# Moving one chunk's attention steps among the first FFN groups of a fused retention and gated FFN kernel

## The chip, the cores and the metric

The kernel runs on one core of a Trainium2 chip. The metric is the device time of one execution in microseconds (us). An execution of the kernel before was also profiled; all times of single instructions below come from that one profile. The engines are named as in it: PE is TensorE (matrix products; PEld is its loading of weights), DVE is VectorE, ACT is ScalarE, POOL is GpSimd, SP is SyncE.

## The reference

Two stages follow each other. The first is a retention recurrence over four sequences of 768 steps with 8 heads of width 64; the second is a feed-forward network (FFN) with a sigmoid gate over the 3072 tokens that result.

```python
gamma = 1.0 - 2.0 ** (-5.0 - np.arange(H))
for t in range(S):
    state = gamma * state + outer(k[:, :, t], v[:, :, t])      # per batch and head, 64 x 64
    y[:, :, t] = scale * q[:, :, t] @ state
x = y.transpose(0, 2, 1, 3).reshape(3072, 512)
out = (sigmoid(x @ w_gate) * (x @ w_val)) @ w_out              # 512 -> 1536 -> 512
```

## The kernel before

**Chunks.** The recurrence is computed in chunks of 128 steps, numbered g = 0 to 23, six for each sequence. A chunk passes through these functions:

- `transposes_early(g)` (L150 to L159): for k and then for q, four TensorE transposes of 128x128 (L158) into PSUM and one ScalarE copy (L159) into the tile `qkT`. `transposes` (L146, L148) does the same with one copy and is used from chunk 4 on.
- `scale_v(g)` (L169): v times a decay table, into `vs`, on VectorE or GpSimd.
- `scores(g)` (L179): eight products of k and q. `masks(g)` (L184, L185): two VectorE products with the causal mask, into `stA` and `stB`.
- `inter(g)` (L191): four products of q with the state of the chunk before, into the PSUM tile `y`.
- `state(g)` (L201): eight products of k and `vs` added to the state. `state_out(g)` (L209): two ScalarE copies of the state into `zbd`.
- `intra(g)` (L215): eight products of `vs` with `stA` and `stB`, added to `y`.
- `y_out(g)` (L223): one VectorE product of `y` with a decay table, into 128 columns of `xT`, the input of the FFN.

**FFN.** Four chunks make an FFN tile t of 512 tokens. `up(t, n1, lo, hi)` computes one of twelve groups for the columns lo to hi: four products with `wg` and four with `wv` (L261), a sigmoid on ScalarE (L265) and a VectorE product (L266) into `hT`. `up_columns` (L275, L280, L281) does several groups for few columns. `down(t, sm, part)` (L292) is half of a 128-row block of the output product, six matmuls; behind the second half ScalarE copies the block (L297), and SP stores it.

**PSUM.** The tiles of tag `ff` rotate through three buffers. `keep_on`, each half of an `up`, the q part of `transposes_early` and each `down` block take the next one in the order of the program. The first product into a buffer waits until its last content has been read.

**Order.** The schedule is manual: each engine runs its instructions in the order in which the program issues them. The lines up to L389 are written out one after the other. `keep_on(n)` (L304) issues n products of the identity with itself into an unused `ff` tile. Behind them the loop over t issues 9 `up` groups and 8 `down` halves for t = 0, numbered 0 to 16, and places the nine steps of chunks 4 to 7 behind the groups named in `place`. The last of these, `step_y(6, 7)`, issues `inter(6)`, `scores(7)`, `state(6)`, `intra(6)`, `state_out(6)`, `masks(7)` and `y_out(6)`. The first group of t = 1 is `up(1, 0, 0, 384)`, which reads the columns of chunks 4, 5 and 6.

**Loads.** The loads of k, q and v (L67, L68, L62), `wg` and `wv` (L81) and `wo` (L85) are issued on GpSimd's queue in a fixed order; a slab of `wg` or `wv` holds two groups.

Of the kernel before, what the change touches and what calls it, by code (L numbers as in the profile page):

```python
# [17 lines left out]
def kernel(  # L18
# [51 lines left out]
    def load_chunk(g):  # L70
        load_kq(g)
        load_v(g, nc.gpsimd)
# [66 lines left out]
    def pair(t, p):  # L139
        return t[:, 2 * p:2 * p + 2, :].rearrange("s h d -> s (h d)")  # L140
# [9 lines left out]
    def transposes_early(g):  # L150
        qkT[g] = at.tile([128, 2 * NP, C], BF16, tag="qkT", name="qkT", bufs=3)
        for i, x in enumerate((kn[g], qn[g])):
            if i:
                tp = pf.tile([128, NP, C], BF16, tag="ff", name="tq", padded_shape=[128, 2 * NP, C])
            else:
                tp = pa.tile([128, NP, C], BF16, tag="tp", name="tp", padded_shape=[128, 2 * NP, C])
            for p in range(NP):
                nc.tensor.transpose(tp[:, p, :], pair(x, p), ident)  # L158
            nc.scalar.activation(qkT[g][:, i * NP:(i + 1) * NP], tp, AX.Copy)  # L159
# [7 lines left out]
    def scale_v(g, eng):  # L167
        vs[g] = ld.tile([C, H, D], BF16, tag="vs", name="vs", bufs=4)
        eng.tensor_tensor(vs[g], vf[g], tabv[:, g % NCH, :].unsqueeze(2).to_broadcast([C, H, D]),  # L169
                          op=ALU.mult)  # L170

    def scores(g):
        t = qkT[g]
        sc[g] = (pa.tile([128, NP, C], F32, tag="sA", name="sA"),
                 pa.tile([128, NP, C], F32, tag="sB", name="sB"))
        for p in range(NP):
            for i in range(2):
                half = slice(i * D, (i + 1) * D)
                nc.tensor.matmul(sc[g][i][:, p, :], t[half, p, :], t[half, NP + p, :], start=True, stop=True)  # L179

    def masks(g):
        stA[g] = at.tile([128, NP, C], BF16, tag="stA", name="stA")
        stB[g] = at.tile([128, NP, C], BF16, tag="stB", name="stB")
        nc.vector.tensor_tensor(stA[g], sc[g][0], causal4, op=ALU.mult)  # L184
        nc.vector.tensor_tensor(stB[g], sc[g][1], causal4, op=ALU.mult)  # L185

    def inter(g):
        y[g] = pa.tile([128, NP, C], F32, tag="y", name="y")
        if g % NCH > 0:
            for p in range(NP):  # L190
                nc.tensor.matmul(y[g][:, p, :], zbd[(g - 1) % 2][:, p, :], qkT[g][:, NP + p, :],  # L191
                                 start=(p == 0), stop=False, skip_group_check=True)

    def state(g):
        b, c = divmod(g, NCH)
        if c == 0:
            zps[b] = pa.tile([128, NP, D], F32, tag="z", name="z", padded_shape=[128, NP, C])
        if c < NCH - 1:
            for p in range(NP):
                for i in range(2):  # L200
                    nc.tensor.matmul(zps[b][i * D:(i + 1) * D, p, :], kn[g][:, 2 * p + i, :], vs[g][:, 2 * p + i, :],  # L201
                                     start=(c == 0 and p == 0), stop=True, skip_group_check=True)

    def state_out(g):
        b, c = divmod(g, NCH)
        if c < NCH - 1:
            for i in range(2):
                half = slice(i * D, (i + 1) * D)
                nc.scalar.copy(zbd[g % 2][half, :, half], zps[b][half])  # L209

    def intra(g):
        first = g % NCH == 0
        for p in range(NP):
            for i, st in enumerate((stA[g], stB[g])):
                nc.tensor.matmul(y[g][i * D:(i + 1) * D, p, :], vs[g][:, 2 * p + i, :], st[:, p, :],  # L215
                                 start=(first and p == 0), stop=True, skip_group_check=True)

    def y_out(g):
        c = g % NCH
        if g % 4 == 0:  # L220
            xT[g // 4] = at.tile([128, NP, 512], BF16, tag="xT", name="xT")
        col = (g % 4) * C
        nc.vector.tensor_tensor(xT[g // 4][:, :, col:col + C], y[g], taby[:, :, c * C:(c + 1) * C], op=ALU.mult)  # L223

    def step_t(g):
        if g < XBAR:
            transposes(g)
        scale_v(g, nc.vector if g < XBAR else nc.gpsimd)

    def step_s(g):  # L230
        scores(g)
        masks(g)
# [21 lines left out]
    def up(t, n1, lo=0, hi=512):  # L254
        if t not in hT:
            hT[t] = ffn.tile([128, NFF, 512], BF16, tag="hT", name="hT", bufs=2)
        ps = []
        for w in (wg, wv):
            u = pf.tile([128, 512], F32, tag="ff", name="ff")
            for kk in range(KT):  # L260
                nc.tensor.matmul(u[:, lo:hi], w[:, kk, n1 * 128:(n1 + 1) * 128], xT[t][:, kk, lo:hi],  # L261
                                 start=(kk == 0), stop=(kk == KT - 1))
            ps.append(u)
        gs = ffn.tile([128, 512], F32, tag="gs", name="gs")
        nc.scalar.activation(gs[:, lo:hi], ps[0][:, lo:hi], AX.Sigmoid)  # L265
        nc.vector.tensor_tensor(hT[t][:, n1, lo:hi], gs[:, lo:hi], ps[1][:, lo:hi], op=ALU.mult)  # L266

    def up_columns(t, n1s, lo, hi):
        n = hi - lo
        ps = []  # L270
        for w in (wg, wv):
            u = pf.tile([128, 512], F32, tag="ff", name="ff")
            for i, n1 in enumerate(n1s):
                for kk in range(KT):
                    nc.tensor.matmul(u[:, i * n:(i + 1) * n], w[:, kk, n1 * 128:(n1 + 1) * 128], xT[t][:, kk, lo:hi],  # L275
                                     start=(kk == 0), stop=(kk == KT - 1))
            ps.append(u[:, :len(n1s) * n])
        gs = ffn.tile([128, 512], F32, tag="gs", name="gs")
        g = gs[:, :len(n1s) * n]
        nc.scalar.activation(g, ps[0], AX.Sigmoid)  # L280
        nc.vector.tensor_tensor(hT[t][:, n1s[0]:n1s[-1] + 1, lo:hi], g.rearrange("p (i n) -> p i n", n=n),  # L281
                                ps[1].rearrange("p (i n) -> p i n", n=n), op=ALU.mult)
# [18 lines left out]
    def keep_on(n):  # L301
        u = pf.tile([128, 512], F32, tag="ff", name="ff")
        for _ in range(n):
            nc.tensor.matmul(u[:, :128], ident, ident, start=True, stop=True)  # L304
# [64 lines left out]
    scores(2)  # L369
    masks(2)  # L370
    inter(2)
    state(2)
    state_out(2)
    keep_on(12)
    intra(2)
    y_out(2)
    scale_v(3, nc.vector)
    transposes_early(3)
    up(0, 0, 0, 384)
    scores(3)  # L380
    masks(3)
    inter(3)
    state(3)
    state_out(3)
    up(0, 1, 0, 384)
    intra(3)
    y_out(3)
    up(0, 2, 0, 384)
    up_columns(0, range(3), 384, 512)  # L389


    def ups(t):
        return [lambda n1=n1: up(t, n1) for n1 in range(NFF)]

    def downs(t):
        return [lambda sm=sm, i=i: down(t, sm, i) for sm in range(4) for i in range(2)]

    for t in range(NT):
        groups, steps, place = ups(t) + downs(t), [], []
        if t == NT - 1:  # L400
            groups[-2:] = [lambda: last_down(t)]
        if t == 0:
            groups = groups[3:]
            steps = [lambda: step_t(4), lambda: step_s(4), lambda: step_y(4), lambda: step_t(5), lambda: step_s(5),
                     lambda: step_t(6), lambda: step_y(5, 6), lambda: step_t(7), lambda: step_y(6, 7)]
            place = [5, 6, 8, 10, 11, 12, 13, 14, 15]
        elif t + 1 < NT:
            steps = attention(t + 1)
            place = [0, 1, 3, 5, 7, 8, 10, 13, 17]
        if t == 1:  # L410
            groups[:2] = [lambda: up(1, 0, 0, 384), lambda: step_y(7), lambda: up(1, 1, 0, 384),
                          lambda: up_columns(1, range(2), 384, 512)]
            place = [p + 2 for p in place]
        if t + 2 < NT:
            for g in range(4 * t + 8, 4 * t + 12):
                load_chunk(g)
        for i, group in enumerate(groups):
            if i == len(groups) - 9:
                for g in range(4 * t + 8, 4 * t + 12):
                    if XBAR <= g < NG:  # L420
                        xbar(g)
            group()
            for p, step in zip(place, steps):
                if p == i:
                    step()
# [30 lines left out]
```

## Time and profile before

| What | us |
|---|---|
| median of 7 runs | 237.27 (237.04 to 237.88) |
| profiled execution | 237.16 |
| its span, first to last instruction | 235.5 |
| PE busy in the span | 225.9 (96%) |
| DVE busy | 104.5 |
| ACT busy | 90.8 |
| POOL busy | 92.1 |

The span is what the instructions of the profile cover; the profiled execution's own time is 1.66 us above it. The granted TensorE clock was 1.000 of full speed in the mean. In a line of the timeline the first number is the start in us from the start of the span, the second the time that the piece covers, then the engine, the line of the kernel, the operation, output and input tiles with their shapes, and the number of instructions; a bracket tells how long the engine had been idle, and what ended the wait. [...]pieces overlap: the cost of a piece in a full stream is the distance from its start to the start of the next.

### The profile page before, as it was taken

To read this page: it belongs to the slowest core of one execution; us is meant where nothing else is said; L and a number is where in the kernel's file an instruction comes from. 1 tells how busy PE (TensorE), PEld (TensorE's weight loads), DVE (VectorE), ACT (ScalarE), POOL (GpSimd) and SP (SyncE) were. 2 spreads that over 40 slices of the span, in tenths; PEclk is the share of its full clock that TensorE was granted. 3 is DMA by queue.
4 is the path that set the end of the run, shared out by engine and by line. 5 is a ranking of instruction groups with operands and counts; after the bars stand their busy time and mean duration, and the time that the engine had idled before them with its cause. 6 is when DMAs were issued, how large, how long until landed. Compare 5 with 4: busy or idle time off the path is not lost.

```text
span 235.5 us, 4300 instructions
## 1 busy us (share of the span) xinstructions
PE 225.9 (96%) x1702; PEld 117.8 (50%) x1728; DVE 104.5 (44%) x178; ACT 90.8 (39%) x173; POOL 92.1 (39%) x111
## 2 busy tenths in 40 slices
PE   6869999999999999999999999999999999999994
PEld 5646544555555554445454444445444554444444
DVE  3566436464656641346641346641346641234301
ACT  7864334335454521334423334223334331333211
POOL 8999874789786428983111001111000000000000
DMA  8999999999999999999992362012100012100022
GB/s 142 184 193 175 197 204 205 189 221 236 224 171 128 147 134 206 254 177 96 135 150 90 91 89 47 1 47 90 45 3 0 0 47 84 50 0 3 0 89 89
DMA packets 77555, 27.27 MB, mean 116 GB/s; under 512 B 65056, under 2 KB 73120, under 8 KB 77536
## 3 DMA queue, kind: packets, MB, share of 16 engines
q0 software_dynamic: 57616, 16.78, 69.8%
q1 hardware_dynamic: 19776, 10.16, 21.3%
q8 instruction: 13, 0.21, 0.4%
q10 hardware_dynamic: 144, 0.07, 0.1%
q14 instruction: 6, 0.05, 0.1%
HBM read 28.31 MB, written 6.29 MB: 147 GB/s over the span
## 4 chain that ended last, share of the span: by engine, by line
PE 89%; POOL 4%; DMA 2%; issue 1%; ACT 1%; DVE 1%; ACTq 0%; POOLq 0%
PE ff L261 52%; PE ff L292 25%; PE sA L179 3%; PE y L215 2%; DMA qn<-in_q_dram 2%; PE y L191 2%; PE z L201 2%; PE tp L146 2%; PE ff L312 1%; POOL vs L169 1%; POOL kn L67 1%; POOL vf L62 1%; POOL qn L68 1%; PE ff L275 1%; ACT ob L297 1%
## 5 line engine op out<-in xcount | busy, mean ns | idle before, releaser
L266 DVE TENSOR_TENSOR hT<-gs,ff 128x512 bf16<-128x512 f32 (+1 forms) x72 | 48.9, 679 | 74.6 <-PE ff L261 73.0
L261 PE MATMUL ff<-xT,wg 128*128 128x512 bf16 (+1 forms) x276 | 71.9, 376 | 0.6
L261 PE MATMUL ff<-xT,wv 128*128 128x512 bf16 (+1 forms) x282 | 72.0, 375 | 0.3
L265 ACT ACTIVATE gs<-ff 128x512 f32<-128x512 f32 (+1 forms) x72 | 42.4, 589 | 67.1 <-PE ff L261 66.6
L292 PE MATMUL ff<-wo,hT 128*128 128x512 bf16 x268 | 62.4, 379 | 0.6 <-issue 0.2
L261 PEld LDWEIGHTS <-wv 128*128 128x128 bf16 x288 | 28.1, 98 | 32.9
L261 PEld LDWEIGHTS <-wg 128*128 128x128 bf16 x288 | 26.6, 98 | 30.0 <-issue 0.4
L292 PEld LDWEIGHTS <-hT 128*128 128x128 bf16 x276 | 25.9, 98 | 30.1
L297 ACT COPY ob<-ff 128x512 f32<-128x512 f32 x23 | 13.5, 586 | 52.3 <-PE ff L292 47.1
L169 POOL TENSOR_TENSOR vs<-vf,tabv 128x512 bf16<-128x512 f32 x14 | 14.5, 1048 | 47.0 <-PE y L215 42.0
L223 DVE TENSOR_TENSOR xT<-y,taby 128x512 bf16<-128x512 f32 x24 | 16.4, 685 | 20.1 <-PE y L215 20.0
L62 POOL DMA_DIRECT2D vf<-in_v_dram x23 | 20.7, 899 | 10.3 <-DMA kn<-in_k_dram 3.5
L67 POOL DMA_DIRECT2D kn<-in_k_dram x23 | 20.8, 906 | 8.0 <-DMA qn<-in_q_dram 3.5
L184 DVE TENSOR_TENSOR stA<-sA,causal 128x512 bf16<-128x512 f32 x24 | 16.5, 687 | 14.2 <-PE sB L179 14.0
L68 POOL DMA_DIRECT2D qn<-in_q_dram x23 | 20.4, 887 | 4.5 <-DMA wo<-in_moe_w_out_dram 2.4
L209 ACT CAST zbd<-z 64x256 bf16<-64x256 f32 x40 | 14.7, 367 | 11.8 <-PE z L201 11.4
L185 DVE TENSOR_TENSOR stB<-sB,causal 128x512 bf16<-128x512 f32 x24 | 16.3, 681 | 0.0
L169 DVE TENSOR_TENSOR vs<-vf,tabv 128x512 bf16<-128x512 f32 x10 | 7.4, 736 | 6.1 <-DMA vf<-in_v_dram 6.1
L215 PE MATMUL y<-stA,vs 128*64 128x128 bf16 x96 | 9.7, 222 | 0.0
L148 ACT ACTIVATE qkT<-tp 128x1024 bf16<-128x1024 bf16 x8 | 8.2, 1025 | 3.5 <-PE tp L146 3.5
L215 PE MATMUL y<-stB,vs 128*64 128x128 bf16 x96 | 9.4, 221 | 0.0
L304 PE MATMUL ff<-ident 128*128 128x128 bf16 x80 | 7.2, 255 | 1.6 <-POOL ident masks.py:199 1.6
(58 smaller groups left out, 123.5 us busy)
## 6 DMA issues: line engine op xcount, KB each, us to landing
vf<-in_v_dram POOLq DMA_DIRECT2D x23, 256.0 KB, 8.6
out_dram<-ob SPq DMA_DIRECT2D x23, 256.0 KB, 2.0
kn<-in_k_dram POOLq DMA_DIRECT2D x23, 128.0 KB, 8.6
qn<-in_q_dram POOLq DMA_DIRECT2D x23, 128.0 KB, 8.6
wg<-in_moe_w_gate_dram POOLq DMA_DIRECT2D x6, 256.0 KB, 6.6
wv<-in_moe_w_val_dram POOLq DMA_DIRECT2D x6, 256.0 KB, 7.0
wo<-in_moe_w_out_dram POOLq DMA_DIRECT2D x4, 384.0 KB, 10.5
kf<-in_k_dram SPq DMA_DIRECT2D x1, 256.0 KB, 3.3
```

The lines of the kernel that those rows point to most:

```text
L62: eng.dma_start(out=vf[g], in_=src(v, g))
L67: nc.gpsimd.dma_start(out=kn[g], in_=src(k, g))
L68: nc.gpsimd.dma_start(out=qn[g], in_=src(q, g))
L169: eng.tensor_tensor(vs[g], vf[g], tabv[:, g % NCH, :].unsqueeze(2).to_broadcast([C, H, D]), op=ALU.mult)
L184: nc.vector.tensor_tensor(stA[g], sc[g][0], causal4, op=ALU.mult)
L185: nc.vector.tensor_tensor(stB[g], sc[g][1], causal4, op=ALU.mult)
L215: nc.tensor.matmul(y[g][i * D:(i + 1) * D, p, :], vs[g][:, 2 * p + i, :], st[:, p, :], start=(first and p == 0), stop=True, skip_group_che ...
L223: nc.vector.tensor_tensor(xT[g // 4][:, :, col:col + C], y[g], taby[:, :, c * C:(c + 1) * C], op=ALU.mult)
L261: nc.tensor.matmul(u[:, lo:hi], w[:, kk, n1 * 128:(n1 + 1) * 128], xT[t][:, kk, lo:hi], start=(kk == 0), stop=(kk == KT - 1))
L265: nc.scalar.activation(gs[:, lo:hi], ps[0][:, lo:hi], AX.Sigmoid)
L266: nc.vector.tensor_tensor(hT[t][:, n1, lo:hi], gs[:, lo:hi], ps[1][:, lo:hi], op=ALU.mult)
L292: nc.tensor.matmul(o, hT[t][:, n1, sm * 128:(sm + 1) * 128], wo[:, n1, :], start=(n1 == 0), stop=(n1 == NFF - 1))
```

## The change

In the part that is written out, the filler products become 14 and move directly behind `inter(2)`, and `intra(2)` moves ahead of `state(2)` and `state_out(2)`. The first FFN group goes ahead of `transposes_early(3)`, the second between it and `scores(3)`, the third between `state_out(3)` and `intra(3)`. In the loop over t = 0, the last six of the nine attention steps go one group later each.

```diff
     inter(2)
+    keep_on(14)
+    intra(2)
     state(2)
     state_out(2)
-    keep_on(12)
-    intra(2)
     y_out(2)
     scale_v(3, nc.vector)
+    up(0, 0, 0, 384)
     transposes_early(3)
-    up(0, 0, 0, 384)
+    up(0, 1, 0, 384)
     scores(3)
     masks(3)
     inter(3)
     state(3)
     state_out(3)
-    up(0, 1, 0, 384)
+    up(0, 2, 0, 384)
     intra(3)
     y_out(3)
-    up(0, 2, 0, 384)
     up_columns(0, range(3), 384, 512)
...
             steps = [lambda: step_t(4), lambda: step_s(4), lambda: step_y(4), lambda: step_t(5), lambda: step_s(5),
                      lambda: step_t(6), lambda: step_y(5, 6), lambda: step_t(7), lambda: step_y(6, 7)]
-            place = [5, 6, 8, 10, 11, 12, 13, 14, 15]
+            place = [5, 6, 8, 11, 12, 13, 14, 15, 16]
```

On PE this is two products more and otherwise the same ones in another order; on VectorE and ScalarE the same instructions in another order; GpSimd and SP issue the same in the same order.

## The prediction

> **What bounds the kernel now.** The page's first part gives PE 225.9 of 235.5 us, and the chain that ended last is 89% PE. So the time is PE's stream of products plus PE's gaps, and an edit that only reorders is worth the gaps it closes less those it opens. I looked next at who PE waited for (the table of waits, PE alone), then at the timeline of PE and DVE around the two edited places. The first place, PE and then DVE:
>
> ```profile
> 15.63 0.22 PE L215 MATMUL y<-stB,vs 128*64 128x128 bf16 x1
> 16.63 0.40 PE L158 MATMUL tp<-ident,kn 128*128 128x128 bf16 x4 [0.78 <-DMA kn<-in_k_dram]
> 17.60 0.40 PE L158 MATMUL tq<-ident,qn 128*128 128x128 bf16 x4 [0.58 <-DMA qn<-in_q_dram]
> 17.83 0.81 PE L261 MATMUL ff<-xT,wg 128*128 128x384 bf16 x4
> 18.48 0.81 PE L261 MATMUL ff<-xT,wv 128*128 128x384 bf16 x4
> ...
> 21.88 0.82 PE L261 MATMUL ff<-xT,wg 128*128 128x384 bf16 x4
> 22.54 0.81 PE L261 MATMUL ff<-xT,wv 128*128 128x384 bf16 x4
> 23.19 0.83 PE L275 MATMUL ff<-xT,wg 128*128 128x128 bf16 x12
> ```
>
> ```profile
> 14.73 0.68 DVE L185 TENSOR_TENSOR stB<-sB,causal 128x512 bf16<-128x512 f32 x1
> 15.95 0.69 DVE L223 TENSOR_TENSOR xT<-y,taby 128x512 bf16<-128x512 f32 x1 [0.54 <-PE y L215]
> 18.48 0.69 DVE L169 TENSOR_TENSOR vs<-vf,tabv 128x512 bf16<-128x512 f32 x1 [1.83 <-DMA vf<-in_v_dram]
> 19.40 0.56 DVE L266 TENSOR_TENSOR hT<-gs,ff 128x384 bf16<-128x384 f32 x1 [0.23 <-PE ff L261]
> ...
> 21.71 0.56 DVE L266 TENSOR_TENSOR hT<-gs,ff 128x384 bf16<-128x384 f32 x1 [0.56 <-PE ff L261]
> 22.19 0.68 DVE L223 TENSOR_TENSOR xT<-y,taby 128x512 bf16<-128x512 f32 x1
> ```
>
> The reader sees PE stand twice for chunk 3's k and q. Counted from start to start, the stream of `intra(2)` is over at 15.69 (15.63 plus one step of 0.06), so the waits are 16.63 - 15.69 = 0.94 and, with four transposes of 0.056 behind 16.63, 17.60 - 16.85 = 0.75: 1.69 us in all. From 17.83 to 23.19 PE doesn't wait: the third group hides `y_out(3)` (22.19 to 22.87).
>
> The second place, the end of FFN tile 0, PE and then DVE:
>
> ```profile
> 53.81 0.23 PE L179 MATMUL sA<-qkT 64*128 64x128 bf16 x1
> ...
> 54.84 1.24 PE L292 MATMUL ff<-wo,hT 128*128 128x512 bf16 x5 [0.16 <-issue]
> 56.18 0.81 PE L261 MATMUL ff<-xT,wg 128*128 128x384 bf16 x4
> ```
>
> ```profile
> 54.24 0.69 DVE L184 TENSOR_TENSOR stA<-sA,causal 128x512 bf16<-128x512 f32 x1 [1.33 <-PE sB L179]
> 54.85 0.68 DVE L185 TENSOR_TENSOR stB<-sB,causal 128x512 bf16<-128x512 f32 x1
> 55.45 0.68 DVE L223 TENSOR_TENSOR xT<-y,taby 128x512 bf16<-128x512 f32 x1
> ```
>
> `scores(7)` start at 53.81; DVE then makes two masks and only third `y_out(6)`, which ends at 56.13; `up(1, 0)` starts at 56.18. The last `down` half lies in that time (six matmuls of 0.216; the first, at about 54.62, has no record, so the "issue" gap is none).
>
> **The change part by part: the first place.** I place the new order on PE with the distances of the rows above: a 384-wide half group 0.65 (17.83 to 18.48), a group 1.30, eight transposes 0.46, `scores` 0.33 with 0.10 lost at the switch to them (18.48 + 0.65 = 19.13, but 19.23), `inter` 0.33, `state` 0.24, `intra` 0.34 with 0.10 at its switch.
>
> *Fillers, `intra(2)`, `state(2)`.* 14 fillers at 0.065 (12 took 0.78) start at 13.5 where `state(2)` waited for `vs`, and end near 14.4. `intra(2)` needs `stB`, which ends at 15.41 in both orders, so it still ends at 15.69: two more fillers cost nothing, hidden by that mask; without that cover they would cost 0.13. `state(2)`, before hidden in the same wait, now stands behind: 0.24 and a switch of 0.05, to 15.98. Its copies on ScalarE end near 17.0, far ahead of `inter(3)`.
>
> *`up(0, 0)`.* It needs `y_out(2)`, 15.95 to 16.64, so it starts at 16.69 (0.05 from DVE's end to PE, as at 56.13 to 56.18). Wait: 0.71. Its weight slabs, issued at 9.07 and 9.88, landed 5.3 and 5.9 later, by 15.8: no wait. It ends at 17.99, by when k and q of chunk 3 are there (17.55). The transposes end at 18.45 and wait for nothing: the two transfers are hidden.
>
> *`up(0, 1)`: a new wait.* `ff` buffers rotate by three. Before, q's transposes stood between fillers and `up(0, 0)`; now they stand behind it. So the second half of `up(0, 1)` falls on the buffer of the second half of `up(0, 0)`, which is read by the VectorE product L266; before, it fell on a buffer that a ScalarE sigmoid frees. On VectorE that L266 is queued behind `scale_v(3)`, which waits for v of chunk 3 until 18.48 and ends at 19.17. L266 of group 0 then runs from about 19.10 to 19.66 (successive DVE pieces overlap by 0.08), though its inputs are there at 18.2. The half would start at 19.10 and starts at 19.71: 0.61. This is the step I'm least sure of. From below it costs 0, if v came 0.6 sooner; from above about 0.8, if L266 follows at the distance of the row (19.40). I take 0.61, because v's transfer is issued by an unchanged queue.
>
> *`scores(3)` to `intra(3)`.* 20.36 + 0.10 + 0.33 + 0.33 + 0.24 = 21.36 for the start of `up(0, 2)`. Its slabs, issued at 14.31 and 15.05, landed after 5.5 and 6.1, at 19.8 and 21.15; they are needed at 21.36 and 22.01: nothing, though without the new wait the second would have only 0.26 in hand. `intra(3)` runs from 22.76 to 23.10; its masks ended near 22.4.
>
> *`y_out(3)` without its cover.* The third group used to lie between it and `up_columns`; now `up_columns` stands right behind `intra(3)`. `hT` of group 2 is ahead on DVE: its product ends 0.81 after 22.01, so L266 runs 22.93 to 23.49, and `y_out(3)` 23.41 to 24.09. `up_columns` starts at 24.14: a wait of 1.04.
>
> Sum: PE's work from 15.69 to `up_columns` is 5.80 in both (3 x 1.30 + 0.46 + 0.33 + 0.33 + 0.24 + 0.34 + 0.20), and 23.19 - 15.69 = 7.50 leaves the 1.69 of waits. After: 5.80 + 0.29 for `state(2)` + 0.71 + 0.61 + 1.04 = 8.45. **The first place costs 0.95 us.** The gap for the transfers goes, but v, on the same queue, is late next, and y's copies are uncovered.
>
> **The second place.** Six steps move behind the next `down` half, each 6 x 0.216 = 1.30 later, with their distances to each other kept. One half thereby moves from behind `step_y(6, 7)` to ahead of chunk 5's transposes, and nothing lies between `step_y(6, 7)` and `up(1, 0)`. From the start of `scores(7)` to `up(1, 0)` DVE needs what it needs now, 56.18 - 53.81 = 2.37: two masks and `y_out(6)`. PE has 54.62 - 53.81 = 0.81 of work there; before it had 1.30 more and stood 0.26; now it stands 1.56. **Cost: 1.30.** ScalarE's copy of the output block (0.59 at 56.16 before) goes ahead of the two state copies, over before they are due. The store behind it on SP is issued earlier with nothing behind it; GpSimd's queue has the same order, and its loads of chunks 5 to 7 are issued by 45.3, ahead of the moved steps.
>
> A small gain lies against this. Chunk 5's q transposes start at 44.68 where a full stream would have put them at 44.57; q, issued at 33.43, landed after 11.2, at 44.63. With 0.95 of delay this wait is gone: -0.11. Moving the step by another 1.30 gains nothing more.
>
> **Sum.** 0.95 + 1.30 - 0.11 = 2.14. The profiled execution took 237.16 with a span of 235.5; I let the 1.66 around it stand: span 237.6, time 239.3. The median stands 0.11 above the profiled time, so **239.4**. Behind 62 us no gap of PE is long enough to absorb any of it: of its 0.2 us waits or more, all but the first instants' are at the places named, bar one of 0.3 at 61.37 which moves along.
>
> [...]New gaps raise a question about the clock. The windows of the profile give, for the thinnest stretch,
>
> ```profile
> 16.00:17.90 1.90, 0.70 (x9) 0.53 (x10) 0.65 (x1) 0.60 (x1) 1.90 (x3) 1.00 1.24 214
> ```
>
> PE busy 0.70 of 1.90 us and the granted clock still 1.00. [...] I take the row: the new gaps (0.71, 0.61, 1.04, 1.56) are spread further apart than the 0.94 and 0.75 which the clock survived, but 1.56 alone is longer than any that the row shows.
>
> **The rivals.**
>
> *v's wait isn't felt.* If `scale_v(3)` is out of the way sooner, `up(0, 1)` doesn't stop: 239.4 - 0.6 = 238.8. For it: k, q and v come 0.9 apart, and a slightly earlier v counts in full. Against: DVE's 1.83 of idle ended by v's transfer.
>
> *The first place does what its order says.* Neither v nor `y_out(3)` is felt; only 0.71 and 0.29 are left of 1.69, so -0.69, and 1.30 - 0.11 at the second place: 237.27 + 0.50 = 237.8. Against: `y_out(3)` can't start until the product is over, and nothing is between.
>
> *Faster: copies of y don't hold PE.* One mechanism at three places: if the columns of `xT` were free for PE without waiting for L223, 0.71 + 1.04 + 1.56 = 3.31 would go, for 236.1. It decides for faster when over 2.14 + 0.47 = 2.61 of the 3.31 isn't paid. Against: 0.05 between DVE's end at 56.13 and PE's start; each of these groups reads the columns just written.
>
> [...]
>
> *It does nothing.* Waits are exchanged one for one, 237.3; for this 2.14 would have to be made good elsewhere, and PE has no such gap.
>
> **How the numbers follow.** The chances: 0.68 for my sum, 0.12 for v, 0.07 for the useful first place, 0.06 for the clock, 0.04 for faster, 0.03 for nothing. About 0.2% (0.47 us) is what a measurement of this kernel can tell from no change. Slower has 0.68 + 0.12 + 0.06 and half of the useful first place, which lies at the border: 0.90; within 0.2% the other half and nothing: 0.06; faster 0.04. The range leaves out the last four cases, 0.20: from 238.3 (v's case less 0.5 for a shorter copy wait) to 240.2 (the sum, plus 0.2 for L266 at its row's distance, plus 0.6 for switches that I left out).
>
> **What would show it.** `up(0, 0)` starts near 16.7, with no wait on k or q of chunk 3. The second half of `up(0, 1)` starts near 19.7 with a DVE wait. `up_columns` starts near 24.1 after 1.0 us of idle behind L223. `up(1, 0)` starts 2.4 behind `scores(7)`, after 1.5 us of idle. The clock stays 1.00. I'm wrong if `up_columns` starts ahead of 23.2, or if PE's gap ahead of `up(1, 0)` is under 1 us.

## The result and the profile after

The changed kernel takes 239.41 us (median; the middle of the prediction was 239.4). The ratio to the kernel before is 1.0069, with a 95% interval of 1.0049 to 1.009: slower. The profiled execution took 239.15 us with a span of 237.4, that is 1.9 us more span than before. In these comparisons the median of the kernel before is some 237.65 and no longer 237.27, in part because in 39 of 145 executions of it the mean granted TensorE clock is 0.991 to 0.993 (the other 106 are at 0.998 or more, called full clock here, and have a median of 237.5); the experiments come back to that.

Who PE waited for after the change, from the table of waits (us in total, times, longest), the lines that are new:

```profile
PE ff L261 <- DVE xT L223: 2.2, 2, 1.5
PE ff L275 <- DVE xT L223: 1.0, 1, 1.0
PE y L215 <- DVE stB L185: 0.4, 1, 0.4
PE ff L261 <- DVE hT L266: 0.3, 1, 0.3
PE y L215 <- DVE stA L184: 0.2, 1, 0.2
```

All are waits for VectorE. The two of L215 (`intra(2)` for its masks, 0.6) stand where `state(2)` used to wait 0.65 for `vs`, so they cost nothing more; the other three are 3.5 us together. No transposes of chunk 3 are in the table any more. The first place in the timeline of PE:

```profile
15.58 0.22 PE L215 MATMUL y<-stB,vs 128*64 128x128 bf16 x1
15.61 0.31 PE L201 MATMUL z<-vs,kn 128*64 128x64 bf16 x8
16.65 0.81 PE L261 MATMUL ff<-xT,wg 128*128 128x384 bf16 x4 [0.73 <-DVE xT L223]
17.30 0.81 PE L261 MATMUL ff<-xT,wv 128*128 128x384 bf16 x4
17.95 0.39 PE L158 MATMUL tp<-ident,kn 128*128 128x128 bf16 x4
18.17 0.39 PE L158 MATMUL tq<-ident,qn 128*128 128x128 bf16 x4
18.40 0.81 PE L261 MATMUL ff<-xT,wg 128*128 128x384 bf16 x4
19.54 0.81 PE L261 MATMUL ff<-xT,wv 128*128 128x384 bf16 x4 [0.33 <-DVE hT L266]
...
21.85 0.81 PE L261 MATMUL ff<-xT,wv 128*128 128x384 bf16 x4
23.98 0.83 PE L275 MATMUL ff<-xT,wg 128*128 128x128 bf16 x12 [0.97 <-DVE xT L223]
```

and of VectorE:

```profile
15.91 0.69 DVE L223 TENSOR_TENSOR xT<-y,taby 128x512 bf16<-128x512 f32 x1 [0.54 <-PE y L215]
18.33 0.69 DVE L169 TENSOR_TENSOR vs<-vf,tabv 128x512 bf16<-128x512 f32 x1 [1.73 <-DMA vf<-in_v_dram]
18.94 0.55 DVE L266 TENSOR_TENSOR hT<-gs,ff 128x384 bf16<-128x384 f32 x1
...
22.77 0.55 DVE L266 TENSOR_TENSOR hT<-gs,ff 128x384 bf16<-128x384 f32 x1 [0.56 <-PE ff L261]
23.24 0.68 DVE L223 TENSOR_TENSOR xT<-y,taby 128x512 bf16<-128x512 f32 x1
```

The first group runs while k and q arrive, and the transposes at 17.95 wait for nothing. The product of group 0 (18.94) stands behind `scale_v(3)` (18.33), which v's transfer releases; its end at 19.49 lets PE start at 19.54 what would have started at 18.40 + 0.65 = 19.05 (the pieces at 16.65, 17.30 and 17.95 start 0.65 apart, too, though the first two cover 0.81 each). At the end `up_columns` starts 0.06 behind `y_out(3)`, at 23.98 instead of 23.19.

The second place, PE, then `y_out(6)` on VectorE:

```profile
55.78 0.23 PE L179 MATMUL sA<-qkT 64*128 64x128 bf16 x1
...
58.15 0.81 PE L261 MATMUL ff<-xT,wg 128*128 128x384 bf16 x4 [1.50 <-DVE xT L223]
```

```profile
57.41 0.68 DVE L223 TENSOR_TENSOR xT<-y,taby 128x512 bf16<-128x512 f32 x1
```

From `scores(7)` to `up(1, 0)` it is 2.37 as before, but 1.50 of it is idle. From `up_columns` to `up(1, 0)` the kernel before took 56.18 - 23.19 = 32.99; this one takes 58.15 - 23.98 = 34.17. So the loss is 0.79 at the first place and 1.18 from there to the end of the second, 1.97 in all; behind 58 us nearly nothing is lost or made good (the spans differ by 1.9).

### The profile page after: what moved, and what is told of

Its sections match the earlier page's. It is cut to its first block, busy times and chain, and to the rows that moved or that the text cites. A ratio compares the mean times of both kernels' runs of the same rounds, so it can differ in the third digit from the quotient of the medians.

```text
span 237.4 us, 4305 instructions
## 1 busy us (share of the span) xinstructions
PE 225.5 (95%) x1705; PEld 118.1 (50%) x1730; DVE 103.6 (44%) x178; ACT 90.8 (38%) x173; POOL 92.0 (39%) x111
## 4 chain that ended last, share of the span: by engine, by line
PE 88%; POOL 5%; DMA 2%; issue 2%; DVE 1%; ACT 1%; ACTq 0%; POOLq 0%; DVEq 0%
PE ff L261 50%; PE ff L292 26%; PE sA L179 3%; DMA vf<-in_v_dram 2%; PE y L215 2%; PE y L191 2%; PE z L201 2%; PE tp L146 2%; PE ff L312 1%; POOL qn L68 1%; POOL kn L67 1%; POOL vs L169 1%; POOL vf L62 1%; PE ff L275 1%; DVE xT L223 1%
## 5 line engine op out<-in xcount | busy, mean ns | idle before, releaser
L215 PE MATMUL y<-stA,vs 128*64 128x128 bf16 x96 | 9.6, 221 | 0.2 <-DVE stA L184 0.2
L215 PE MATMUL y<-stB,vs 128*64 128x128 bf16 x96 | 9.5, 221 | 0.4 <-DVE stB L185 0.4
```

## Experiments

Ratios are to the kernel before, with 95% intervals. The kernels of one group ran on the same chip; between groups the chip differs, and the changed kernel was not run again in them, so differences from its 239.41 may be across chips.

**First group: the parts of the change.** Each place alone, and each of the two costs of the first place taken away.

`first_place_only` is the changed kernel with

```diff
-            place = [5, 6, 8, 11, 12, 13, 14, 15, 16]
+            place = [5, 6, 8, 10, 11, 12, 13, 14, 15]
```

> The changed kernel with the six late attention steps back behind the groups of the kernel before. My account: the first place alone costs what its profile shows, up_columns 0.8 us later than before, less the 0.1 us for which chunk 5's q was waited for: +0.7 us on the kernel before (ratio 1.003). up(1, 0) follows a down half and stands only 0.26 us. Rival (the first place does what its order says, all of the loss is in the moved steps): up_columns would be earlier than before, and the ratio 1.000 or below.

Measured: 237.95 us, ratio 0.9994 (0.9967 to 1.0021). Its profile:

```profile
23.96 0.83 PE L275 MATMUL ff<-xT,wg 128*128 128x128 bf16 x12 [0.97 <-DVE xT L223]
...
56.83 0.81 PE L261 MATMUL ff<-xT,wg 128*128 128x384 bf16 x4
```

In the profile it is as expected: `up_columns` 0.77 later than before, and 32.87 from there to `up(1, 0)`, 0.12 less than before, which is chunk 5's q. The rival, that `up_columns` would come earlier, has fallen. But the ratio doesn't show the 0.7 us; the second group explains it.

`second_place_only` is the kernel before with the opposite edit of `place`.

> The kernel before with only the six steps moved one group later. My account: +1.3 us for the down half that no longer covers y_out(6), less 0.1 us for chunk 5's q: +1.2 us (ratio 1.005), with 1.5 us of idle ahead of up(1, 0) that ends with L223. Rival (copies of y don't hold PE): no such idle, ratio 1.000 or below.

Measured: 238.47 us, ratio 1.0032 (1.0011 to 1.0054).

```profile
16.87 0.56 PE L158 MATMUL tp<-ident,kn 128*128 128x128 bf16 x4 [1.02 <-DMA kn<-in_k_dram]
17.70 0.61 PE L158 MATMUL tq<-ident,qn 128*128 128x128 bf16 x4 [0.27 <-DMA qn<-in_q_dram]
...
24.59 0.83 PE L275 MATMUL ff<-xT,wg 128*128 128x128 bf16 x12
...
58.76 0.81 PE L261 MATMUL ff<-xT,wg 128*128 128x384 bf16 x4 [1.50 <-DVE xT L223]
```

The 1.50 us of idle is there, and from `up_columns` to `up(1, 0)` it is 34.17, 1.18 more than before, to the hundredth as in the changed kernel. But `up_columns` is at 24.59, although nothing ahead of it differs from the kernel before (23.19). The windows of this profile, ahead of it and in it (busy time and counts of PE, PEld, DVE, ACT and POOL, then the granted clock, the DMA share and GB/s), say why:

```profile
16.00:18.00 2.00, 0.86 (x8) 0.60 (x9) 0.65 (x1) 0.53 (x1) 2.00 (x3) 0.74 1.14 198
18.00:20.00 2.00, 2.00 (x9) 1.02 (x8) 0.69 (x1) 1.03 (x3) 2.00 (x4) 0.50 1.15 144
20.00:22.00 2.00, 2.00 (x26) 1.11 (x25) 1.20 (x3) 0.43 (x2) 2.00 (x3) 0.91 1.34 173
```

and the same windows of the kernel before:

```profile
16.00:18.00 2.00, 0.80 (x10) 0.56 (x11) 0.65 (x1) 0.60 (x1) 2.00 (x3) 1.00 1.23 210
18.00:20.00 2.00, 2.00 (x26) 1.15 (x26) 1.29 (x3) 1.09 (x2) 2.00 (x4) 1.00 1.27 165
```

The clock fell to half at about 17, behind the wait for k (PE idle for 1.02 us), and stayed there for some 3.4 us (0.26, 0.50 and 0.09 are missing from 1.00 over 2 us each, 1.70 in all, and at half clock 0.50 is missing); PE then did 9 matmuls where it does 26. `up_columns` is 1.40 us later than in the kernel before: 0.10 of it is q, whose transposes start at 17.70 and not at 17.60, and the other 1.30 is the clock, since PE waits for nothing from there on.

`v_after_first_group` is the changed kernel with

```diff
-    scale_v(3, nc.vector)
     up(0, 0, 0, 384)
+    scale_v(3, nc.vector)
```

> The changed kernel with scale_v(3) issued behind up(0, 0), so that on VectorE the product of group 0 isn't queued behind the wait for v. My account: the second half of up(0, 1) no longer waits, and up_columns comes 0.5 us earlier than in the changed kernel: -0.5 us (ratio to the kernel before about 1.005 instead of 1.007). Rival (the wait isn't felt, or the next one takes its place): up_columns at 24.0 as in the changed kernel, no difference.

Measured: 238.95 us, ratio 1.0045 (1.0029 to 1.0061), 0.46 less than the changed kernel.

```profile
18.45 0.81 PE L261 MATMUL ff<-xT,wg 128*128 128x384 bf16 x4
19.10 0.81 PE L261 MATMUL ff<-xT,wv 128*128 128x384 bf16 x4
...
23.54 0.83 PE L275 MATMUL ff<-xT,wg 128*128 128x128 bf16 x12 [0.97 <-DVE xT L223]
```

The halves of `up(0, 1)` now follow at 0.65; the wait is gone and no other takes its place. That the cause was the order on VectorE is shown.

`cover_for_y3` is the changed kernel with a fourth group behind `y_out(3)`; as one group less is left for the loop, the numbers in `place` go down by one:

```diff
     y_out(3)
-    up_columns(0, range(3), 384, 512)
+    up(0, 3, 0, 384)
+    up_columns(0, range(4), 384, 512)
...
-            groups = groups[3:]
+            groups = groups[4:]
...
-            place = [5, 6, 8, 11, 12, 13, 14, 15, 16]
+            place = [4, 5, 7, 10, 11, 12, 13, 14, 15]
```

> The changed kernel with a fourth group, up(0, 3, 0, 384), between y_out(3) and up_columns, which then does the last 128 columns of four groups; the nine steps stay ahead of the same groups. My account: the 0.97 us of idle ahead of up_columns goes, at a cost of 8 matmuls that are split in two (about 0.02 us): -0.95 us (ratio to the kernel before about 1.003). Rival (the product is held by something else, such as wv's slab or the hT product ahead of it on VectorE): the idle moves ahead of the fourth group, and little is gained.

Measured: 238.42 us, ratio 1.0016 (0.9992 to 1.0039), 0.99 less than the changed kernel.

```profile
22.05 0.81 PE L261 MATMUL ff<-xT,wv 128*128 128x384 bf16 x4
23.14 0.82 PE L261 MATMUL ff<-xT,wg 128*128 128x384 bf16 x4
...
24.45 1.06 PE L275 MATMUL ff<-xT,wg 128*128 128x128 bf16 x16
```

From the third group's second half to the fourth group it is 1.09, which is 0.65 and `intra(3)`; `up_columns` follows without idle.

**Second group: the clock, the order of `state(2)`, and all covers together.** If thin occupation around the waits for k and q (PE busy 0.86 of 2 us in the profile with the fall, 0.80 in that of the kernel before) makes the clock fall, filling one of them should stop it. `fillers_for_k3` is the kernel before with

```diff
     scale_v(3, nc.vector)
+    keep_on(12)
     transposes_early(3)
```

> The kernel before with 12 more filler products between y_out(2) and transposes_early(3), in the wait for chunk 3's k (0.94 us from start to start; the fillers need 0.78 and delay nothing that isn't waiting). Of 59 executions of the kernel before, 15 show a mean granted clock of 0.991 to 0.993 and take some 1.4 us more (median 238.9 against 237.5). Theory (the clock falls because PE stands thinly occupied around the waits for k and q): no or hardly any execution at 0.993; an execution at full clock as before, 237.5 (within 0.2 us); the ratio about 0.998. Rival (the falls come from elsewhere in the kernel, or are the chip's own): a quarter of the executions at 0.993 as before.

```profile
15.80 0.84 PE L304 MATMUL ff<-ident 128*128 128x128 bf16 x12
16.59 0.40 PE L158 MATMUL tp<-ident,kn 128*128 128x128 bf16 x4
17.49 0.40 PE L158 MATMUL tq<-ident,qn 128*128 128x128 bf16 x4 [0.50 <-DMA qn<-in_q_dram]
```

Measured: 237.51 us, ratio 0.9994 (0.9976 to 1.0012). None of its 14 executions had a low mean clock. In the three groups together 39 of 145 executions of the kernel before show a mean clock below 0.995, 13 of 51 in this group. Were it no different here, none in 14 would have a chance of between 1 and 2 in 100. Of the other kernels in which fillers or the first group stand where PE waited for k and q, 2 of 149 executions show it, and these two took 3.8 and 6.7 us more than their medians, far more than a fall costs. `second_place_only`, which leaves the waits as they were, shows it in 6 of 22. So the falls hang on this stretch. Which executions have one stays open: only one profile shows a fall, and in it k came 0.24 later than in the profile of the kernel before. What they cost: executions of the kernel before at full clock have a median of 237.5 us, those at low clock about 238.9. The interval of this ratio is too wide to show the gain in the time itself; the expected 0.998 lies in it, and so does 1.

At full clock the changed kernel is 239.41 - 237.50 = 1.9 above the kernel before, as in the two profiles (1.97). The ratio of 1.0069 is lower because the falls are in the times of the kernel before: about 0.27 x 1.4 = 0.4 us on average, which the change wins back. The same hides the loss in `first_place_only`: 237.95 is 0.45 above 237.50, and no execution of its 14 had a low clock. The executions of `second_place_only` at full clock have a median of 238.39, 0.89 above. In the profiles the two places alone add up to the whole (0.65 and 1.18 later at `up(1, 0)`, and 0.12 for chunk 5's q that both count); in these medians they come to 1.3 of the 1.9 us, and why is open.

`state_ahead_of_intra` is the changed kernel with `state(2)`, `state_out(2)` and then 12 fillers back ahead of `intra(2)`.

> The changed kernel with state(2) and state_out(2) back ahead of 12 fillers and intra(2). My account: state(2) now lies in the wait for y_out(2), which intra(2) starts at the same time in both orders, so the wait grows from 0.73 to about 1.0 and the sum stays: up_columns at the same time (0.1 us), 239.4. Rival (0.29 us is a cost of its own): 0.3 us faster than the changed kernel.

Measured: 239.28 us, ratio 1.0063 (1.0041 to 1.0086), in 6 executions 0.13 less than the changed kernel.

```profile
16.23 0.22 PE L215 MATMUL y<-stB,vs 128*64 128x128 bf16 x1
17.30 0.81 PE L261 MATMUL ff<-xT,wg 128*128 128x384 bf16 x4 [0.85 <-DVE xT L223]
```

From the last product of `intra(2)` to the first group it is 1.07, and in the changed kernel 16.65 - 15.58 = 1.07 too: the 0.24 of `state(2)` lies inside the wait for `y_out(2)` and costs nothing. (In this execution `intra(2)` came 0.65 later and PE then no longer stood for v, so `up_columns`, at 24.14, doesn't tell the two apart.)

`all_covered` joins the edits of `v_after_first_group` and `cover_for_y3`, with chunk 5 one half later than before, chunk 6's transposes beside chunk 5's scores, and `step_y(6, 7)` ahead of the last half (against `cover_for_y3`):

```diff
-            place = [4, 5, 7, 10, 11, 12, 13, 14, 15]
+            place = [4, 5, 7, 10, 11, 11, 12, 13, 14]
```

> The changed kernel with scale_v(3) behind up(0, 0), a fourth group ahead of up_columns, chunk 5's transposes still one group later than before, chunk 6's transposes moved up beside chunk 5's scores, and step_y(6, 7) back ahead of the last down half. My account: v's wait (0.5) and y_out(3)'s (0.97) go, and the half covers y_out(6) again (1.3): from 239.4 to 236.7, that is 0.65 us ahead of the kernel before at the first place and 0.1 at chunk 5's q: 236.7 to 236.8 against 237.5, ratio 0.997 or less. Rival (the early gain is given back to a later transfer): 237.5.

Measured: 237.33 us, ratio 0.9973 (0.9959 to 0.9986): faster than both kernels, though only 0.2 below the 237.5 of the kernel before at full clock. The profiled execution took 236.39 with a span of 234.7:

```profile
22.50 0.82 PE L261 MATMUL ff<-xT,wg 128*128 128x384 bf16 x4
...
55.40 0.81 PE L261 MATMUL ff<-xT,wg 128*128 128x384 bf16 x4
```

`up(1, 0)` starts at 55.40 instead of 56.18, 0.78 earlier, as worked out. But the 22 executions, all at full clock, spread from 236.39 to 237.91, and the median is 0.6 above the expected 236.7.

`chunk5_at_its_old_place` is `all_covered` with `place = [4, 5, 7, 9, 10, 11, 12, 13, 14]`.

> As all_covered, but the attention steps of chunks 5 to 7 behind the groups of the kernel before. My account: chunk 5's transposes now come 0.65 us sooner than in the kernel before, q of chunk 5 doesn't, and PE stands 0.7 to 0.8 us for it where the kernel before stood 0.1: 237.4 to 237.5, the gain of the first place is gone. Rival (the transfer comes sooner too, or isn't waited for): as all_covered, 236.7.

Measured: 237.48 us, ratio 0.9987 (0.9973 to 1.0002).

```profile
43.90 0.39 PE L146 MATMUL tp<-ident,kn 128*128 128x128 bf16 x4
44.80 0.40 PE L146 MATMUL tp<-ident,qn 128*128 128x128 bf16 x4 [0.51 <-DMA qn<-in_q_dram]
```

From k's to q's transposes it is 0.90 instead of 0.22: chunk 5's q holds PE for 0.68, and the gain of the first place is gone: `up(1, 0)` starts at 56.31, in the kernel before at 56.18. Here the time won early was lost again in the wait for a transfer that didn't come sooner (q's transposes at 44.80, in the kernel before at 44.68). In the medians the two kernels differ by only 0.15, since `all_covered` didn't reach its 236.7 either.

**Third group: the spread of `all_covered`.** In its profile chunk 6's q landed at 47.3 (issued at 36.6, 10.7 on the way) and was needed at 47.38. `chunk6_later_too` gives it room, with

```diff
-            place = [4, 5, 7, 10, 11, 11, 12, 13, 14]
+            place = [4, 5, 7, 10, 11, 12, 13, 13, 14]
```

> As all_covered, but chunk 6's transposes and step_y(5, 6) also one down half later, with chunk 7's transposes right behind step_y(5, 6); step_y(6, 7) stays ahead of the last half. In the profile of all_covered chunk 6's q landed at 47.3 and its transposes needed it at 47.37, with nothing in hand; its 22 executions lie between 236.4 and 237.9. Theory (in many executions that q is later and PE stands for it): nearly all executions near 236.5 to 236.9, ratio about 0.996. Rival (the spread comes from the start of the kernel or elsewhere): the same spread, median 237.3, ratio 0.997.

Measured: 236.60 us, ratio 0.995 (0.9931 to 0.9969), the fastest of all. Its 14 executions lie between 236.38 and 237.21; in the profile chunk 6's q landed at 48.0 and was needed at 48.92. The kernel before at full clock has a median of 237.43 in this group, so 0.8 us is the new order, near the 0.75 that was worked out for `all_covered`.

`all_covered` was run again beside it.

> all_covered again, on the same chip as chunk6_later_too. Theory (chunk 6's q): a wait for it shows where this execution takes over 237, none where it takes 236.5. Rival: an execution over 237 shows the extra time in the first 16 us or elsewhere.

Measured: 236.99 us, ratio 0.997 (0.9951 to 0.999), executions from 236.26 to 238.35. Its profile fell on the shortest of them, and in it chunk 6's q came just in time (36.8 + 10.4 = 47.2; the transposes of q ran at 47.23). So moving chunk 6 narrows the spread, as the theory has it, but no profile shows the wait for its q itself; that part is argued, not shown.

## Why the prediction was right

**The first place, forecast 0.95, measured 0.79.** Of the difference, 0.05 is only that `intra(2)` ended at 15.64 in this profile and not at 15.69. The steps hold one by one. `up(0, 0)` started at 16.65 (forecast 16.69), k and q were no longer waited for, `up_columns` started at 23.98 (24.14). The new wait behind `scale_v(3)` was the term that was mis-sized: 0.49 instead of 0.61, because v was taken up at 18.33 and not at 18.48. The transfer sets the second half of `up(0, 1)` at 19.5 in two profiles that reached this group 0.24 apart (19.54 in the changed kernel, 19.52 in `first_place_only`), so the size of the wait depends on how early the kernel got there: 0.49 and 0.23, and nothing in `state_ahead_of_intra`. The wait for `y_out(3)` was 1.05 between starts, against 1.04. That `state(2)` costs 0.29 was a matter of accounts only (the 0.05 in it for a switch was an estimate; `state(2)` starts 0.03 behind the last start of `intra(2)`): the forecast let the wait for `y_out(2)` shrink by the same amount, and in both orders it is 1.07 from `intra(2)` to the first group.

**The second place, forecast 1.30, less 0.11 for chunk 5's q: measured 1.18.** The half no longer covers two masks and `y_out(6)`, and PE stands 1.50. The two places alone give the same numbers in their profiles as the whole.

**The rivals.** That v's wait isn't felt, that the first place does what its order says, and that copies of y don't hold PE: each is refuted by a bracket in the profile after, the first only for executions that get there as early as this one. `v_after_first_group` and `cover_for_y3` show the price of the first two.

**The clock.** Here the working was wrong, though the sum wasn't moved by it. The forecast read the granted clock of 1.00 in the thinnest stretch of the kernel before as proof that gaps of 0.94 and 0.75 are harmless, and looked for a fall only in the changed kernel; the 0.06 that it gave to one was the author's estimate. That row was one execution. In 39 of 145 executions the kernel before has a low clock, and `fillers_for_k3` ties this to just that stretch; the changed kernel has it in none of 17. The profile of `second_place_only`, with the clock at 0.50 behind 1.02 us of idle in that stretch, speaks against the reading of the row. The missing term spoke for the change and not against it: a fall cost the kernel before some 1.4 us, so it is a gain of some 0.4 us on average. Without it the ratio would be near 1.008 (239.41 to 237.50) and not 1.0069; the forecast implies 1.009 (239.4 to 237.27). The forecast met the median of the changed kernel because it was made against an execution of the kernel before at full clock.

**Luck.** That the median is met to 0.01 us is luck. The profiled execution came out 0.15 below the forecast (239.15 for 239.3), and the median lies 0.26 above it where 0.11 was taken over from the kernel before.

## What to carry to other kernels

When work is moved to cover one wait, list what it covered where it stood: here three groups had hidden ScalarE's copy of the transposes, the masks and `y_out(3)`, and a `down` half had hidden `y_out(6)`; in `chunk6_later_too` a fourth group had to be brought in, and the half put back, for a gain to come of it. With rotating buffers, look at which engine frees the buffer that the moved step now falls on, and what that engine has queued ahead of it (here 0.49 us behind `scale_v(3)`). And look at the steps that wait for a transfer behind a gain: with chunk 5's left where they were, its q held PE for 0.68 us, and the gain of the first place was gone.

## What was not expected of the hardware

The mean TensorE clock was low in 39 of 145 executions of the kernel before. In the one profile that shows a fall (`second_place_only`), the clock was at half for about 3.4 us, behind a stretch in which PE had no idle longer than 1.02 us; in 16 of the 22 executions of that program, and in 106 of the 145, the mean stayed at 0.998 or more. A longer idle elsewhere did not do it: behind the 1.50 us ahead of `up(1, 0)` the clock stayed at 1.00 (58.2 to 62 us) in the profile of the changed kernel, and none of its 17 executions had a low mean. Twelve filler products of 0.065 us in one of the two waits for k and q were enough that no fall was seen in 14 executions. The one profile of the kernel before, at 1.00 in this stretch, didn't show the falls; the mean clocks of its 145 executions did.
